# Query-key-norm attention and a soft mixture of experts: seven tokens of a head per partition, heads in fours, and fp32 loads of q, k and v by the hardware queue

## The chip, the cores and the metric

One core of a Trainium2 chip runs the whole program. The metric is the device time of one execution in microseconds (us), as the median of several. The profile's span is some 2 us shorter than that time (300.6 of 302.37 us before). Engines: PE is the matrix engine and PEld its weight loads, ACT evaluates functions (here the exponentials), DVE and POOL are the two elementwise engines, SP does nothing in these traces but issue transfers.

## The reference, cut to what matters

```python
# q, k, v: (8, 12, 448, 64) fp32
def rmsnorm(x, g):
    rms = np.sqrt(np.mean(x * x, axis=-1, keepdims=True) + 1e-06)
    return x / rms * g
q_n, k_n = rmsnorm(q, g_q), rmsnorm(k, g_k)
attn = softmax(q_n @ k_n.T / sqrt(64)) @ v            # 96 heads
x = attn.transpose(0, 2, 1, 3).reshape(3584, 768)
logits = x @ phi                                      # phi: (768, 32)
d = softmax(logits, axis=0); slot_input = d.T @ x     # 8 experts, 4 slots each
h = relu(slot_input[e] @ w1[e]); slot_out[e] = h @ w2[e]   # w1 768x1024, w2 1024x768
out = softmax(logits, axis=1) @ slot_out              # (3584, 768) fp32
```

The kernel reads 33 MB of q, k and v and 50 MB of expert weights, all fp32 (and 4.7 MB of the weights a second time, from a bf16 scratch), and computes in bf16. Attention fills most of the time; the expert weights (16 matrices of 3.1 MB) are fetched under it, so that the experts can start as soon as the last head is done.

## The kernel before

It puts four tokens of a head on each of 112 partitions (448 = 112 x 4) and works on pairs of heads. In this kernel all loads with a cast go through GpSimd's software queue (q0 of the page): q, k, v and the weights arrive in bf16 in one queue.

```python
P = 112; SI = 4; HU = 6; GU = HU // 2      # units of six heads, three pairs each
place("raw", 2 * HU * SI * D, 4)           # q and k of four units
place("vraw", HU * SI * D, 3)

def load(u, h0=0, h1=HU):                  # one unit, cast to bf16 on the way
    b, hb = u // 2, (u % 2) * HU
    for t, src in ((0, q), (1, k)):
        nc.gpsimd.dma_start(out=rawunit(u)[:, t, h0:h1],
                            in_=src[b, hb + h0:hb + h1].rearrange("h (p si) d -> p h (si d)", p=P))

def loadw(i):                              # one expert matrix
    if i in scratch:                       # the last three go by way of DRAM
        nc.sync.dma_start(out=wplace[i], in_=scratch[i])
    else:
        nc.gpsimd.dma_start(out=wt[i], in_=wsrc(i))

for g in range(-3, NG + 4):                # one pair of heads per step
    ...
    elif g + 6 < NG:
        square(g + 6)                      # ACT, or POOL for every third pair
    if 0 <= g + 2 < NG:
        scaleqk(g + 2)                     # POOL: q and k times 1/rms; frees raw
    ...
    if g >= 0 and g % GU == 1:
        u = g // GU
        if u + 4 < NU:
            load(u + 4)                    # first needed by square(3u + 12), at g = 3u + 6
        if u + 3 < NU:
            loadv(u + 3)
```

A unit is asked for five steps, 5 x 4.5 = 22.5 us, before its first use (21.7 to 23.9 us in the trace, from unit 5 on).

The softmax here doesn't subtract the row's maximum and nothing guards it: scores larger than these inputs give would overflow.

## Time and profile before

| | before |
|---|---|
| time | 300.09 us, median of 3 (298.52 to 300.27) |
| span of the profiled run (that execution took 302.37 us) | 300.6 us |
| first exponential starts, last one ends | 15.4, 230.24 us |
| first expert matmul | 239.08 us |
| experts, from there to the transposes of their outputs | 26.85 us |
| pace of attention | 9.0 us per four heads |

The views that bound the kernel (engines, windows, groups, chain) stand in the prediction below. The first two lines are from the table of waits: who waited for what; us in total, times, longest.

```profile
ACT arena L172 <- DMA arena<-in_k_dram: 6.0, 3, 3.6
...
POOL arena L199 <- DMA arena<-in_v_dram: 1.6, 1, 1.6
```

The next are from the page's tables of queues (packets, MB, share of 16 engines) and of transfers (number, KB each, median us from the request to the landing).

```profile
q0 software_dynamic: 48464, 41.73, 90.4%
q1 hardware_dynamic: 3056, 15.73, 12.9%
...
arena<-in_q_dram POOLq DMA_DIRECT2D x15, 336.0 KB, 6.7
arena<-in_k_dram POOLq DMA_DIRECT2D x15, 336.0 KB, 7.7
```

The hardware queue q1 carries only the output and the reloads from scratch. A load of q or k takes 6.7 or 7.7 us to land in the median (11.0 at most); the four waits of the first fence all lie before 21 us. (The 336 KB are what lands, in bf16; in fp32, each load reads 672 KB.)

### The profile page before, as it was taken

How to read it: one execution, taken by the hardware profiler on the slowest of the kernel's cores; microseconds unless marked ns; L12 is line 12 of the kernel's file. 1: busy time of each engine (PE TensorE's matmuls, PEld its weight loads, DVE VectorE, ACT ScalarE, POOL GpSimd, SP SyncE). 2: the span in 40 equal slices, each digit the busy share in tenths (PEclk: the TensorE clock that was granted, in tenths of full speed). 3: DMA queues.
4: the chain of work that ended last, by engine and by line, in shares of the span. 5: the costliest groups of instructions: out<-in, count | busy, mean ns of one | idle time of the engine just before them, and what ended most of it. 6: DMA issues, size and time to landing. Idle time of an engine off the chain costs nothing. (4 is left out here: it accounts for less than half of the span.)

```text
span 300.6 us, 8905 instructions
## 1 busy us (share of the span) xinstructions
PE 241.5 (80%) x3828; PEld 182.8 (61%) x3828; DVE 205.8 (68%) x407; ACT 216.2 (72%) x283; POOL 205.6 (68%) x233
## 2 busy tenths in 40 slices
PE   7469878989797898979789897989996776989900
PEld 3137556767685676758567675867875676854300
DVE  3575867978889897988989788888675410138800
ACT  3498996989998998999899899979986000026700
POOL 8879999989998998999999999977930000000000
PEclk9756995988999999999999989979999555555555
DMA  6999999999999999999999999999799991009996
GB/s 75 147 147 173 204 188 206 192 175 175 198 167 185 175 197 150 151 206 195 190 166 205 193 201 134 164 194 210 117 185 211 311 409 50 4 2 396 411 413 248
DMA packets 51558, 58.02 MB, mean 193 GB/s; under 512 B 2496, under 2 KB 42944, under 8 KB 51136
## 3 DMA queue, kind: packets, MB, share of 16 engines
q0 software_dynamic: 48464, 41.73, 90.4%
q1 hardware_dynamic: 3056, 15.73, 12.9%
q8 instruction: 30, 0.49, 0.6%
q14 instruction: 8, 0.07, 0.1%
HBM read 88.18 MB, written 15.73 MB: 346 GB/s over the span
## 5 line engine op out<-in xcount | busy, mean ns | idle before, releaser
L230 ACT ACTIVATE arena<-sc 112x896 bf16<-112x896 f32 x192 | 162.9, 916 | 14.1 <-PE sc L229 13.9
L229 PE MATMUL sc<-arena 128*112 128x448 bf16 x384 | 113.4, 379 | 15.4 <-ACT arena L230 13.3
L190 POOL TENSOR_TENSOR arena<-arena,rs 112x512 bf16<-112x512 bf16 x96 | 99.1, 1053 | 3.6 <-ACT rs L184 3.4
L240 PEld LDWEIGHTS <-arena 112*128 112x128 bf16 x1536 | 68.1, 100 | 28.5 <-issue 5.3
L178 DVE TENSOR_REDUCE ss<-arena 112x16 f32<-112x1024 f32 x48 | 58.4, 1219 | 26.4 <-ACT arena L172 21.7
L240 PE MATMUL ov<-arena 112*128 112x65 bf16 x1536 | 73.2, 197 | 1.8 <-DVE arena L252 1.4
L229 PEld LDWEIGHTS <-arena 128*112 128x112 bf16 x384 | 43.7, 137 | 21.5 <-issue 15.4
L172 ACT ACTIVATE arena<-arena 112x1024 f32<-112x1024 bf16 x34 | 35.8, 1052 | 6.1 <-DMA arena<-in_k_dram 6.0
L458 ACT ACTIVATE wown<-op,arena 128x768 f32<-128x768 f32 x14 | 12.4, 900 | 37.8 <-PE op L455 37.8
L199 POOL COPY arena<-arena 112x512 bf16<-112x512 bf16 x48 | 29.0, 604 | 13.1 <-PE ov L240 11.5
L218 PEld LDWEIGHTS <-arena 112*128 112x128 bf16 x384 | 25.6, 104 | 16.9 <-POOL arena L190 9.4
L218 PE MATMUL qkTp<-ident,arena 112*128 112x112 bf16 x384 | 30.5, 225 | 6.4 <-POOL arena L190 6.3
L252 DVE TENSOR_TENSOR arena<-ov,rd 128x512 bf16<-128x512 f32 x48 | 33.2, 691 | 1.7
L265 DVE COPY arena<-xTp 128x512 bf16<-128x512 bf16 x48 | 20.4, 425 | 9.6 <-PE xTp L264 8.5
L170 POOL TENSOR_TENSOR arena<-arena 112x1024 f32<-112x1024 bf16 x14 | 26.7, 1909 | 0.2
L219 DVE TENSOR_SCALAR arena<-qkTp,gg 128x448 bf16<-128x448 bf16 x48 | 21.5, 449 | 1.9 <-PE qkTp L218 1.3
L264 PE MATMUL xTp<-ident,arena 128*128 128x128 bf16 x192 | 19.1, 222 | 1.1 <-DVE arena L252 1.1
L221 DVE COPY arena<-qkTp 64x448 bf16<-64x448 bf16 x48 | 18.9, 395 | 1.2
L220 DVE COPY arena<-qkTp 64x448 bf16<-64x448 bf16 x48 | 17.9, 373 | 0.0
L460 DVE TENSOR_SCALAR wown<-op,arena 128x768 f32<-128x768 f32 x14 | 14.2, 1017 | 4.6 <-PE op L455 4.4
L454 PE MATMUL op<-arena,eT 32*128 32x512 bf16 x28 | 16.0, 617 | 1.4 <-ACT wown L458 0.7
L124 POOL DMA_DIRECT2D arena<-in_q_dram x18 | 14.3, 792 | 0.9 <-POOLq L478 0.9
(61 smaller groups left out, 208.2 us busy)
## 6 DMA issues: line engine op xcount, KB each, us to landing
wown<-in_moe_w_dram POOLq DMA_DIRECT2D x10, 1536.0 KB, 13.8
out_dram<-wown SPq DMA_DIRECT2D x12, 768.0 KB, 8.5
arena<-in_v_dram POOLq DMA_DIRECT2D x16, 336.0 KB, 8.9
arena<-in_q_dram POOLq DMA_DIRECT2D x15, 336.0 KB, 6.7
arena<-in_k_dram POOLq DMA_DIRECT2D x15, 336.0 KB, 7.7
scr<-in_moe_w_dram POOLq DMA_DIRECT2D x3, 1536.0 KB, 11.4
arena<-in_moe_w_dram POOLq DMA_DIRECT2D x3, 1536.0 KB, 13.1
arena<-scr SPq DMA_DIRECT2D x2, 1536.0 KB, 12.5
```

The costliest lines, as they stand in the source:

```text
L170: nc.gpsimd.tensor_tensor(sq, rawpair(p), rawpair(p), op=MUL)
L172: nc.scalar.activation(out=sq, in_=rawpair(p), func=ACTF.Square)
L178: nc.vector.reduce_sum(sss[p // GU][:, p % GU], at("sq", p).bitcast(F32).rearrange("p (r d) -> p r d", d=D), axis=AX)
L190: nc.gpsimd.tensor_tensor(qkn[:, t], rawpair(p)[:, t].rearrange("p h (s d) -> p s h d", d=D), rs[:, t].to_broadcast([P, SI, 2, D]), op=MUL)
L199: nc.gpsimd.tensor_copy(vext(p)[:, :, :, :D], vr[:, 2 * hp:2 * hp + 2])
L218: nc.tensor.transpose(pt[:, t, si * P:(si + 1) * P], qkn[:, t, si], ident[:P, :P])
L219: nc.vector.tensor_scalar(qT(p), pt[:, 0], gg, None, op0=MUL)
L229: nc.tensor.matmul(sc[:P, hh, :S], kT(p)[:, hh, i * P:(i + 1) * P], qT(p), start=True, stop=True)
L230: nc.scalar.activation(out=attn(p, i), in_=sc[:P, :, :S], func=ACTF.Exp, scale=0.125)
L240: nc.tensor.matmul(ovs[p][:, hh, c * (D + 1):(c + 1) * (D + 1)], attn(p, sik)[:, hh, C0[c]:C0[c] + 128], vext(p)[:, hh, sik, :D + 1], star ...
L252: nc.vector.tensor_tensor(x(b)[:, :, h * D:(h + 2) * D].rearrange("p c (h d) -> p h c d", d=D), o[:, :, :, :D], rd.to_broadcast([128, 2, 4 ...
L265: nc.vector.tensor_copy(xT(dc), xp)
```

## The change

Its intent: with 112 of 128 partitions in use, an eighth of every elementwise instruction is wasted (an exponential of 896 columns takes 916 ns on 112 partitions here). With seven tokens per partition, two heads fill 128 partitions (2 x 448 = 128 x 7), and a quad of four heads takes two such rows. q, k and v are loaded as fp32, without a cast; SP issues the loads on the hardware queue, and GpSimd is rid of 40 us of issuing (52 issues, 14.3, 13.5 and 12.4 us before). The keys come in chunks of 128; the fourth, of 64, is shared by two heads, which makes 7 exponentials per quad in place of 8. The buffers for q and k hold fp32 now, and there is one for each of three quads. The core of the diff:

```diff
-    place("raw", 2 * HU * SI * D, 4)
-    place("vraw", HU * SI * D, 3)
+    place("raw", 2 * 2 * 2 * NT * D, 3)
+    place("vraw", 2 * 2 * NT * D, 2)
 ...
-            nc.gpsimd.dma_start(out=rawunit(u)[:, t, h0:h1],
-                                in_=src[b, hb + h0:hb + h1].rearrange("h (p si) d -> p h (si d)", p=P))
+        src = (q, k)[t][Q // QB, Q % QB * 4:Q % QB * 4 + 4].rearrange("h t d -> (h t) d")
+        nc.sync.dma_start(out=raw(Q)[:, t], in_=src.rearrange("(r p s) d -> p r (s d)", r=2, s=NT))
 ...
+    def loadv(Q):                          # four transfers, of 1024- and 768-byte rows
+        for r in range(2):
+            ...
+            nc.sync.dma_start(out=vraw(Q)[0:64, ...], in_=src[:, :, :m])
+            nc.sync.dma_start(out=vraw(Q)[64:128, ...], in_=src[:, :, m:])
 ...
-        nc.vector.tensor_copy(eT[...].rearrange("n (p s) -> n s p", s=SI), ...)   # stride 4 elements
+        nc.vector.tensor_copy(eT[...].rearrange("n (p s) -> n s p", s=NT), ...)   # stride 7 elements
 ...
+    for Q in range(NQ + 2):                # the order within one quad, cut
+        if Q + 4 < NQ: load(Q + 4, 0); load(Q + 4, 1)      # SP
+        square(Q + 3, 0); square(Q + 3, 1, True)           # q on ACT, k on POOL
+        scaleqk(Q + 2, 0)                                  # POOL
+        vcopy(Q + 1); scaleqk(Q + 2, 1)                    # POOL
+        loadv(Q + 3)                                       # SP
+        while wnext < NPRE and Q >= wnext * 9 // 5: loadw(wnext); wnext += 1   # software queue
```

## The prediction

> **What bounds the kernel now.** I read the whole page first, then a table of windows, the chain of waits, and the groups of instructions.
>
> ```profile
> PE 241.5 (80%) x3828; PEld 182.8 (61%) x3828; DVE 205.8 (68%) x407; ACT 216.2 (72%) x283; POOL 205.6 (68%) x233
> ```
>
> No engine is full over the span, because the span has stages. The windows (busy time of each engine in each stretch) separate them:
>
> ```profile
> 0.00:15.00 15.00, 9.48 (x40) 3.88 (x40) 6.42 (x17) 6.00 (x9) 12.60 (x21) 0.87 0.92 111
> ...
> 120.00:150.00 30.00, 25.75 (x414) 19.84 (x413) 26.67 (x53) 28.37 (x38) 29.26 (x32) 1.00 1.18 184
> ...
> 250.00:262.00 12.00, 9.97 (x367) 9.90 (x367) 1.31 (x7) 0.00 (x0) 0.00 (x0) 0.50 0.02 5
> 262.00:280.00 18.00, 15.79 (x158) 9.08 (x156) 10.54 (x14) 8.42 (x10) 0.00 (x0) 0.50 0.53 212
> ```
>
> After the length come PE, PEld, DVE, ACT and POOL busy, PE clock, DMA share, GB/s. From about 20 to 230 us is attention: ACT 95% and POOL 98% busy, DVE 89%. ACT and POOL are both nearly full, so taking work from one alone would gain little. The last 60 us (expert layers, output) have nothing of the change in them. The chain of waits gives the pace: the router of two successive batches, six head pairs apart.
>
> ```profile
> 163.62 0.59 PE lg L271 x24
> ...
> 190.62 0.59 PE lg L271 x24
> ```
>
> That is 27.0 us for six pairs: 4.5 us per pair, 9.0 per four heads (a quad). 24 quads make 216 us. The groups that fill it:
>
> ```profile
> L230 ACT ACTIVATE arena<-sc 112x896 bf16<-112x896 f32 x192 | 162.9, 916 | 14.1 <-PE sc L229 13.9
> L190 POOL TENSOR_TENSOR arena<-arena,rs 112x512 bf16<-112x512 bf16 x96 | 99.1, 1053 | 3.6 <-ACT rs L184 3.4
> L178 DVE TENSOR_REDUCE ss<-arena 112x16 f32<-112x1024 f32 x48 | 58.4, 1219 | 26.4 <-ACT arena L172 21.7
> L172 ACT ACTIVATE arena<-arena 112x1024 f32<-112x1024 bf16 x34 | 35.8, 1052 | 6.1 <-DMA arena<-in_k_dram 6.0
> L199 POOL COPY arena<-arena 112x512 bf16<-112x512 bf16 x48 | 29.0, 604 | 13.1 <-PE ov L240 11.5
> L170 POOL TENSOR_TENSOR arena<-arena 112x1024 f32<-112x1024 bf16 x14 | 26.7, 1909 | 0.2
> L124 POOL DMA_DIRECT2D arena<-in_q_dram x18 | 14.3, 792 | 0.9 <-POOLq L478 0.9
> ```
>
> Every one of the ACT, DVE and POOL rows works on 112 partitions; an instruction's time depends on its columns, so an eighth of each is wasted. Back to back an exponential takes 162.9/192 = 0.848 us, less than its own 916 ns, because neighbours overlap. POOL also spends 18+18+16 issues of about 0.78 us, 40 us, on casting q/k/v loads.
>
> [...]512 columns take 425 ns in the bf16 transpose copy, 691 ns in the fp32 normalisation. [...]the trace's bf16 forms have 1.86 (1909/1024) and 2.06 (1053/512). It does not show all-fp32 inputs, which the change introduces: my largest unknown.[...]
>
> **The change, per quad (two pairs before, one quad after).**
>
> ACT. Before: 8 exponentials x 0.848 = 6.8; squares 34/24 x 1.05 = 1.5; logarithm and exponential of the norms and the router's exponential about 0.5. Sum 8.8 of 9.0. After: 168 exponentials in all, 7 x 0.848 = 5.94; [...]one logarithm/exponential pair about 0.5; router 0.1. Sum 7.5. Saved 1.3.
>
> DVE. Before: sums 2 x 1.22, query copies 2 x 0.45, key copies 2 x 0.77, transposed output 2 x 0.43, norms 2 x 0.90, router 1.6 per batch, /3 = 0.54. Sum 8.1. After: [...]key copies 2 x about 0.62; transposed output 0.69; norms unchanged 1.79; router 0.54. Sum 7.1.
>
> POOL. Before: scales 4 x 1.05 = 4.2, squares 14/24 x 1.91 = 1.1, v copies 1.2, q/k/v issues 40/24 = 1.7, weight issues 0.5. Sum 8.7. After: two scales and one square, 896 columns of fp32 each. The bf16 slope (1909-1053)/512 = 1.67 ns gives 1.05 + 384 x 1.67 = 1.69 us[...]. The v copy becomes four instructions (two of 384 columns, two of 128 on half the partitions): about 1.5, more than before, since each pays its fixed cost. Weight issues 0.55. Sum 7.7, with a span from 7.1 to 8.1.
>
> PE. The trace's busy hours have a pair of score matmuls at 0.40 us, an output matmul of 65 columns at about 0.033 and a transpose at 0.05. Before: 16 scores 3.2, 64 outputs 2.1, 24 transposes 1.3, router 0.55: 7.2. After: 14 scores 2.8, 48 outputs of 65 and 8 of 130 columns 2.1, 23 transposes 1.3, router 0.55: 6.75. Not the bound at full clock.
>
> DMA. The bytes read stay 88 MB. Before, attention reads about twice the 184 GB/s that it lands, some 370; the peak slices land 210, so 420. A quad needs 1.38 MB of q/k/v and on average 1.7 MB of weights: 3.1 MB in 8 us is 385 GB/s, close under that.
>
> Pace. ACT alone was busy for 8.8 of 9.0. With ACT at 7.5, POOL at 7.7 and DVE at 7.1, in program order and within 8% of each other, I allow 5% of waiting: 8.05 us per quad. The last three quads have no squares left: 7.3.
>
> Start. Before, the first exponential ran at 15.4 us. After: q and k of the first quad (0.9 MB) by about 5 us; two squares, sums and norms to 7.8; scale 9; transposes and copies 11.7. But both squares and the norm of the second quad stand ahead of the first exponential on ACT, and their row sums stand behind the copies on DVE: 14.5. The first quad carries three extra squares and two norms, and POOL's backlog: it ends at 27.4.
>
> Sum: 27.4 + 20 x 8.05 + 3 x 7.3 = 210.3 for the last exponential. The chain from there to the first expert matmul (last outputs, norm, transposes, router, its copies) took 239.1 - 230.2 = 8.9 before; slightly less after, 8.3: 218.6. The expert layers and output took 300.6 - 239.1 = 61.5 and are unchanged; I add 0.7 for weights that come late. 280.8 of span, so 280 us.
>
> **Rivals.**
> 1. *POOL becomes the bound.* If an all-fp32 operation takes 2.0 us or more, POOL needs 8.1, and the pace is 8.3 to 8.4: +6, about 287. For it: POOL's present 98%[...], four copies in place of two. Against it: 40 us of issues leave POOL.
> 2. *The weights come late.* The change asks for seven weight matrices (3.1 MB each to read) in quads 17 to 22, with the last q/k/v: some 26 MB, 65 us at 400 GB/s. These begin near 163 us and end near 228, the reloads from scratch near 238, while the experts want the last ones from 231 to 241. One interruption more makes 3 to 8 us: 284 to 288. Before, the loads were over at 250 and expert work ran to 265, so there was slack; most of it goes.
> [...]
> 4. *ACT sets a clean pace* of 7.6 with no added waits: about 271.
>
> **Range and chances.** The pace carries nearly everything: 0.3 us per quad is 7 us. Rivals 1 and 2 push up, rival 4 down. 271 to 291, eight times in ten. Faster by over 2% means under 294.1; slower would need a pace over 9.2, which only a serious stall of loads could make. Faster 0.91, same 0.07, slower 0.02.
>
> **What would show it.** Right: the exponentials 168, about 142 us; the all-fp32 POOL rows near 1.9 us; fp32 sums 1.085 us; query copy near 0.68 us; first exponential near 14.5, last near 210, first expert matmul near 219; three router marks 24 us apart. Wrong: a POOL row over 2.1 us with POOL at 98%; ACT waiting for scores for more than 10% of attention; the key copies over 0.9 us; gaps of more than 1 us between expert layers beyond those of before, which point to weights; or squares that wait for loads in mid-attention.

Passages that rested on figures from outside are cut, terms of the forecast's sum among them: one square on ACT, the sums and the query copy on DVE, the two scales and the square on POOL. With them the sums per quad came to 7.5, 7.1 and 7.7 us; without them the terms left give 6.54, 4.26 and 2.05. So 0.95, 2.85 and 5.6 us, and with them the 8.05 of the pace and the 280.8 of the span, were the author's estimates and rest in part on what no trace had shown. The trace after has 945 ns for the square on ACT, 1085 for each of the two sums, 676 for the query copy, 1713 for each scale and 1682 for the square on POOL. The terms that stand without a source measure 617 ns (key copies, 0.62) and 680 (transposed output, 0.69); the 1.9 us near the end for POOL's fp32 rows is such an estimate too. Where a number's subject is cut with it, the 1.86 and 2.06 are POOL's, in ns an element. Also cut is the third rival: that the long copies out of PSUM become slower, for about 290 us. Two statements stand that the traces show with these numbers. Time goes by columns and not by partitions: an exponential of 896 columns took 916 ns on 112 partitions and 914 on 128, and POOL's products of 512 and 1024 columns 1053 and 1909 ns. And each copy of v has a fixed cost: in the trace after they take 501 and 507 ns for 384 columns, and still 288 and 292 for 128.

## The result, and the profile after

The changed kernel took 330.61 us (median of 4 runs, 329.9 to 331.05) beside 299.97 of the kernel before on the same chip: a ratio of 1.103, 95% interval 1.0987 to 1.1072. Ratios here are the mean time of one kernel's fast runs over that of the other's of the same rounds, so they are not quite the ratio of the medians. It is correct.

| | before | predicted | after |
|---|---|---|---|
| span | 300.6 | 280.8 | 329.2 |
| first exponential starts | 15.4 | 14.5 | 16.52 |
| last exponential ends | 230.24 | 210.3 | 261.7 |
| first expert matmul | 239.08 | 218.6 | 270.36 |
| us per quad in the middle | 9.0 | 8.05 | 10.51 |

(The pace after is the time between ACT's squares of quads 4 and 23, over 19 quads.) Everything was lost in attention. Its end moved by 31.5 us; what follows the first expert matmul gave back 2.7, most of it among the experts (24.4 us in place of 26.85), and the span grew by 28.6.

The engines' busy time, and the window that the prediction showed of before:

```profile
PE 234.6 (71%) x3564; PEld 167.0 (51%) x3564; DVE 192.0 (58%) x315; ACT 193.6 (59%) x268; POOL 164.4 (50%) x187
```

```profile
120.00:150.00 30.00, 16.82 (x244) 12.00 (x242) 17.23 (x27) 16.30 (x23) 17.23 (x19) 0.92 1.04 238
```

In these 30 us ACT is busy for 16.3 (28.4 before), POOL for 17.2 (29.3 before), DVE for 17.2: no engine is the bound. (These are 30 bad microseconds, with two long stalls in them. From 16 to 262 us ACT is busy 71% of the time, POOL 65% and DVE 64%.) The work did shrink, as the groups show (busy us, mean ns of one, then idle time before them and what ended it):

```profile
L252 ACT ACTIVATE arena<-sc 128x896 bf16<-128x896 f32 x168 | 147.4, 914 | 31.8 <-PE sc L251 31.1
...
L195 DVE TENSOR_REDUCE ss<-arena 128x14 f32<-128x896 f32 x48 | 52.0, 1085 | 67.7 <-ACT arena L189 59.9
L207 POOL TENSOR_TENSOR arena<-arena,rs 128x896 bf16<-128x896 f32 x47 | 80.5, 1713 | 13.1 <-ACT rs L200 6.9
L187 POOL TENSOR_TENSOR arena<-arena 128x896 f32<-128x896 f32 x21 | 35.3, 1682 | 67.4 <-DMA arena<-in_k_dram 27.5
...
L189 ACT ACTIVATE arena<-arena 128x896 f32<-128x896 f32 x27 | 25.5, 945 | 37.3 <-DMA arena<-in_q_dram 35.3
...
L319 DVE COPY eT<-eTp 32x448 bf16<-32x448 bf16 x8 | 15.2, 1901 | 0.2
```

The last two columns are the news. The squares of q (L189) and of k (L187) stood behind 37.3 and 67.4 us of idle time, and what ended most of it was a load. The table of waits names them (all but one wait of 2.2 us for q lie in mid-attention):

```profile
ACT arena L189 <- DMA arena<-in_q_dram: 35.3, 11, 6.7
...
POOL arena L187 <- DMA arena<-in_k_dram: 27.5, 6, 6.7
...
POOL arena L187 <- DMA arena<-in_v_dram: 17.9, 3, 7.7
```

The last line needs care, as a square of k reads no v. The profile infers what ended a wait from the last semaphore event before it, and that can be the wrong one. In all 13 waits of L187 (named after k, v, PE or DVE), the square starts 0.1 to 0.2 us after the load of its own k has landed; in the three of the last line, k lands at 90.90, 187.69 and 220.80 us and the squares start at 91.04, 187.83 and 220.94. So all 67.4 us of L187 are waits for k, and with L189's the squares wait 104.7 us for loads. Waits of squares are counted in this way below.

The shares of the chain that ended last, by engine, before and then after:

```profile
PE 26%; ACT 14%; DVE 5%; issue 3%; ACTq 0%
```

```profile
DMA 31%; PE 30%; DVE 11%; ACT 10%; POOL 8%; issue 4%; SPq 2%; ACTq 0%; POOLq 0%
```

Transfers now hold 31% of the span on the chain. Before they held none, but there the chain could be followed back only to 141 us, so it says nothing of the first half. The queues and the transfers:

```profile
q1 hardware_dynamic: 29616, 48.77, 47.1%
q0 software_dynamic: 15376, 25.22, 43.2%
...
arena<-in_q_dram SPq DMA_DIRECT2D x24, 448.0 KB, 9.1
arena<-in_k_dram SPq DMA_DIRECT2D x24, 448.0 KB, 10.6
```

q, k and v lie on q1 now, the weights alone on q0, and a load takes 9 to 11 us. Here is one stall in order of time (start, us, engine, what; in brackets the idle time before it and what ended that), first from SP's timeline, then from ACT's:

```profile
125.54 0.61 SPq L129 DMA_DIRECT2D arena<-in_v_dram  x1
126.20 0.60 SPq L130 DMA_DIRECT2D arena<-in_v_dram  x1
126.85 0.60 SPq L129 DMA_DIRECT2D arena<-in_v_dram  x1
127.55 0.59 SPq L130 DMA_DIRECT2D arena<-in_v_dram  x1
128.24 0.54 SPq L118 DMA_DIRECT2D arena<-in_q_dram  x1
```

```profile
137.76 0.90 ACT L252 ACTIVATE arena<-sc 128x896 bf16<-128x896 f32 x1
145.35 0.95 ACT L189 ACTIVATE arena<-arena 128x896 f32<-128x896 f32 x1 [6.68 <-DMA arena<-in_q_dram]
```

SP issues four loads of v, 0.6 us each, when POOL has copied the v before it, and only then the load of q. That one is requested at 128.24 and lands just before 145.35, 17.1 us later; ACT had been idle for 6.68 us.

**The theory.** It has two factors. First, *the lead is short*: load(Q+4) is asked for at the head of step Q and its square stands at the head of step Q+1, one quad later, where before it was 22.5 us. Its buffer is that of quad Q+1, so it cannot be asked for before POOL has scaled that quad, in step Q-1; in the code the loads of v still come between. In the trace POOL keeps the program's order (L187, L207, L214 to L217, L207, three times from 98 to 128 us, with 8.36 us of idle time before the second L187), and that scaling stands behind a square that itself waits for a load, so by the program's order a late load delays the request after next too. From the requests of q to the squares that use them I read a median of 10.1 us and a minimum of 7.8 (quads 6 to 23; the square's own wait is in it). Second, *the landing is long* (9.1 and 10.6 us in the median), because the weights share the 16 DMA engines with it (without them, in e1, it takes 3.9 and 4.8). Counted from the trace's records of transfers, for the stall above (bytes read; packets as the records have them):

```
us        q0 (weights)            q1 (q, k, v)
124-128   334 GB/s, 435 packets    67 GB/s, 221 packets
128-132   251 GB/s, 327 packets   141 GB/s, 330 packets
132-136   301 GB/s, 330 packets    96 GB/s, 326 packets
136-140   327 GB/s, 319 packets    61 GB/s, 320 packets
140-144   222 GB/s, 232 packets   174 GB/s, 443 packets
144-148     0 GB/s,   1 packet    291 GB/s, 991 packets
```

While both queues have work (126 to 142 us here), each gets about the same number of packets, so bytes follow the size of a packet: the weights' rows read 4096 or 3072 bytes, those of q and k 1792, those of v 1024 and 768. Over 30 to 215 us there are 108 microseconds in which each queue starts at least 20 packets of data: 76.8 of the weights and 78.8 of q, k and v in the mean, but 268 GB/s and 111. The equal counts don't hold at every moment: at 123 and 124 us q1 had a request pending and moved nothing. Then, with the weights landed and the loads of the quad too, little is requested: 35 of these 185 us read under 200 GB/s, 15 before. The mean is 314 GB/s, against 359 before in the same stretch. By what rule the engines pass from one queue to the other, the records don't show.

**Rivals.** (a) The loads are late only because they are slow: a fairer share alone would do. (b) Only the order on SP's queue, with v ahead, makes them late. (c) The elementwise work is slower than its busy time shows, so the pace would be near 10 without any load being late.

### The profile page after: what moved, and what is told of

Its sections match the earlier page's. It is cut to its first block, busy times and chain, and to the rows that moved or that the text cites. A ratio compares the mean times of both kernels' runs of the same rounds, so it can differ in the third digit from the quotient of the medians.

```text
span 329.2 us, 8387 instructions
## 1 busy us (share of the span) xinstructions
PE 234.6 (71%) x3564; PEld 167.0 (51%) x3564; DVE 192.0 (58%) x315; ACT 193.6 (59%) x268; POOL 164.4 (50%) x187
## 4 chain that ended last, share of the span: by engine, by line
DMA 31%; PE 30%; DVE 11%; ACT 10%; POOL 8%; issue 4%; SPq 2%; ACTq 0%; POOLq 0%
DMA arena<-in_q_dram 22%; PE ov L265 7%; PE sc L251 7%; ACT arena L252 6%; DMA arena<-in_k_dram 6%; POOL arena L207 4%; DVE eT L319 3%; PE hTp L472 3%; PE soTp L481 3%; PE op L511 3%; DVE arena L276 3%; PE qkTp L225 2%; ACT arena L189 2%; DMA g<-in_g_q_dram 2%; POOL arena L187 2%
## 5 line engine op out<-in xcount | busy, mean ns | idle before, releaser
L252 ACT ACTIVATE arena<-sc 128x896 bf16<-128x896 f32 x168 | 147.4, 914 | 31.8 <-PE sc L251 31.1
L251 PE MATMUL sc<-arena 128*128 128x448 bf16 x336 | 101.6, 388 | 39.1 <-ACT arena L252 38.4
L265 PEld LDWEIGHTS <-arena 128*128 128x128 bf16 x1344 | 64.9, 104 | 63.3 <-DVE arena L276 32.2
L265 PE MATMUL ov<-arena 128*128 128x65 bf16 (+1 forms) x1344 | 72.6, 207 | 27.8 <-DVE arena L276 27.7
L195 DVE TENSOR_REDUCE ss<-arena 128x14 f32<-128x896 f32 x48 | 52.0, 1085 | 67.7 <-ACT arena L189 59.9
L207 POOL TENSOR_TENSOR arena<-arena,rs 128x896 bf16<-128x896 f32 x47 | 80.5, 1713 | 13.1 <-ACT rs L200 6.9
L187 POOL TENSOR_TENSOR arena<-arena 128x896 f32<-128x896 f32 x21 | 35.3, 1682 | 67.4 <-DMA arena<-in_k_dram 27.5
L251 PEld LDWEIGHTS <-arena 128*128 128x128 bf16 x336 | 26.7, 104 | 43.7 <-issue 41.7
L189 ACT ACTIVATE arena<-arena 128x896 f32<-128x896 f32 x27 | 25.5, 945 | 37.3 <-DMA arena<-in_q_dram 35.3
L225 PE MATMUL qkTp<-ident,arena 128*128 128x128 bf16 x360 | 32.6, 241 | 2.2 <-DVE arena L207 1.1
L515 ACT ACTIVATE wown<-op,arena 128x768 f32<-128x768 f32 x14 | 12.4, 899 | 35.9 <-PE op L512 35.9
L225 PEld LDWEIGHTS <-arena 128*128 128x128 bf16 x360 | 26.2, 109 | 9.7 <-POOL arena L207 3.2
L236 DVE COPY arena<-qkTp 64x896 bf16<-64x896 bf16 x48 | 29.6, 617 | 1.3 <-PE qkTp L225 0.4
L517 DVE TENSOR_SCALAR wown<-op,arena 128x768 f32<-128x768 f32 x14 | 14.2, 1017 | 4.6 <-PE op L512 4.4
L290 DVE COPY arena<-xTp 128x1024 bf16<-128x1024 bf16 x24 | 16.3, 680 | 0.7 <-PE xTp L287 0.7
L287 PE MATMUL xTp<-ident,arena 128*128 128x128 bf16 x192 | 14.6, 219 | 1.4 <-DVE arena L276 1.0
L287 PEld LDWEIGHTS <-arena 128*128 128x128 bf16 x192 | 12.7, 98 | 5.9 <-DVE arena L276 1.2
L319 DVE COPY eT<-eTp 32x448 bf16<-32x448 bf16 x8 | 15.2, 1901 | 0.2
## 6 DMA issues: line engine op xcount, KB each, us to landing
arena<-in_k_dram SPq DMA_DIRECT2D x24, 448.0 KB, 10.6
```

What stands on the lines that cost most here:

```text
L187: nc.gpsimd.tensor_tensor(sq(t), r, r, op=MUL)
L189: nc.scalar.activation(out=sq(t), in_=r, func=ACTF.Square)
L195: nc.vector.reduce_sum(sss[Q][:, t], sq(t).rearrange("p (r d) -> p r d", d=D), axis=AX)
L207: (eng or nc.gpsimd).tensor_tensor(qkn(Q, t).rearrange("p s (r d) -> p s r d", r=2), raw(Q)[:, t].rearrange("p r (s d) -> p s r d", d=D), ...
L225: nc.tensor.transpose(pts[t][:, i], qkn(Q, t)[:, s], ident)
L236: nc.vector.tensor_copy(kT(Q)[r, :, hh].rearrange("p w (s c) -> p w s c", s=NT), pt[r, :, 1 - hh:8 - hh])
```

## The experiments

Twelve kernels ran. "Pace" is always that between ACT's squares of quads 4 and 23, "lead" the median from a request of q to its square, "landing" the median of q and of k. The lead runs to the square as it ran, so the square's own wait is in it. The first six kernels ran once each. The kernel before took 299.4 to 300.0 us beside all of them (medians).

| run | time, us | pace | lead | landing q, k | last exponential ends |
|---|---|---|---|---|---|
| changed kernel | 330.6 | 10.51 | 10.1 | 9.1, 10.6 | 261.7 |
| e1_weights_late | 384.7 | 8.28 | 10.8 | 3.9, 4.8 | 218.9 |
| e3_scale_first | 301.1 | 8.82 | 14.2 | 10.9, 12.6 | 229.6 |
| e4_qk_before_v | 305.2 | 8.86 | 12.7 | 9.2, 8.7 | 234.8 |
| e5_small_packets | 307.0 | 9.01 | 8.2 | 7.6, 8.9 | 233.1 |
| e6_four_buffers_mended | 298.5 | 8.57 | 14.6 | 9.1, 9.7 | 224.0 |
| e7_four_and_scale_first | 305.0 | 8.92 | 22.3 | 11.1, 12.3 | 231.1 |
| e8_plain_eT | 302.3 | 8.78 | 21.0 | 10.9, 12.1 | 226.1 |
| e9_halves_spaced | 292.5 | 8.16 | 16.6 | 10.2, 12.2 | 216.9 |
| e10_three_halves | 295.4 | 8.47 | 11.4 | 9.3, 8.7 | 219.4 |
| e11_four_plain_eT | 298.5 | 8.49 | 14.1 | 9.1, 10.0 | 220.0 |
| e12_one_queue_end | 290.9 | 8.16 | 17.4 | 10.4, 11.9 | 216.4 |

### e1_weights_late: attention without the weights beside it

Every weight load moves behind attention; nothing else changes.

```diff
-        while wnext < NPRE and Q >= wnext * 9 // 5:
+        while wnext < NPRE and Q >= NQ:
             loadw(wnext)
 ...   # the casts to scratch and the loads of the last three steps: all at Q == NQ
```

> All 16 expert weights are requested only after the last quad; buffers, order and q/k/v loads stay as in the changed kernel, whose squares ran 10.5 us per quad apart. Theory A (lead too short: a q/k load can only be requested when the POOL has scaled the quad three before, about one quad ahead of its use, and the landing then takes 9 to 17 us): without weights a q/k pair should land in 4 to 5 us after its request, so the waits for in_q and in_k (65 us in the changed kernel) fall under 10 us, the pace falls to about 8.1 us and the last exponential ends near 218 instead of 258 us. Rival B (bandwidth as such: fp32 landing is too much for the DMA engines): attention would speed up too, but q/k landings would stay near 9 us. Rival C (only the order of requests on the sync queue, behind the v loads, holds it): pace stays at 10 us. The total is no use here: the weights then take some 130 us alone, near 400 us.

Measured: 384.67 us (one run; correct). The total is of no interest, as the weights come afterwards with nothing to hide them. Attention ends at 218.9, at a pace of 8.28.

```profile
arena<-in_q_dram SPq DMA_DIRECT2D x24, 448.0 KB, 3.9
arena<-in_k_dram SPq DMA_DIRECT2D x24, 448.0 KB, 4.8
```

The requests come with the lead of the changed kernel (10.8 us), but land in less than half the time. Squares wait for loads for 8.4 us in all, where they had waited for 104.7. So rival (c) falls: the elementwise work, in this order, runs at 8.28, within 3% of the predicted 8.05, if its data are there. It also shows that the contention is with the weights.

### e2_four_buffers: one more buffer for q and k (failed)

Four quads of raw buffers, one weight fewer that has a place of its own, and load(Q+5) at the head of step Q.

```diff
-    NPRE = 10
+    NPRE = 9
-    place("raw", 2 * 2 * 2 * NT * D, 3)
+    place("raw", 2 * 2 * 2 * NT * D, 4)
-        if Q + 4 < NQ or Q == 0:
-            ...load(Q + 4)
+        for qn in ((3, 4, 5) if Q == 0 else (Q + 5,)):
+            if qn < NQ: load(qn, 0); load(qn, 1)
-        if Q in (NQ - 4, NQ - 3, NQ - 2):
-            loadw(NPRE + Q - (NQ - 4))
+        if Q in (NQ - 5, NQ - 4, NQ - 3, NQ - 2):
+            loadw(NPRE + Q - (NQ - 5))
```

> Four buffers of raw q/k in place of three (one own weight place given up for the room), each load requested one quad earlier, weights in the loop as before. Theory A: two quads of lead (about 16 us) cover nearly every landing, waits for in_q and in_k fall from 65 to under 15 us, pace 8.2 to 8.6, total 283 to 293 us. Rival B: bandwidth binds, so the landings only get longer, pace stays near 10, total 320 to 330 us. Rival D ([...]q/k/v cannot get their 170 GB/s on average): a part of the waits stays, 300 to 315 us.

The result was wrong (relative error 0.077), and it is my mistake: the weights that are loaded into spent buffers of q and k started one step too early, and one overwrote the last quad before it was scaled. POOL waited 25.0 us for that weight, so the 314.38 us say nothing. From quad 4 to 20 the pace was 8.59. Mended as e6 below.

### e3_scale_first: free the buffer sooner

Three buffers stay. POOL scales quad Q+2 before it squares quad Q+3, and the load into the freed buffer follows at once.

```diff
+        elif Q + 2 < NQ:                   # head of step Q
+            scaleqk(Q + 2, 0)
+            scaleqk(Q + 2, 1)
+            if Q + 5 < NQ:
+                load(Q + 5, 0)
+                load(Q + 5, 1)
 ...   # the two scaleqk(Q + 2) later in the step go
```

> Three buffers as in the changed kernel; the POOL scales quad Q+2 at the start of quad Q instead of after the square of quad Q+3, which waits for a load, and the load of quad Q+5 is requested right behind it. Theory A says that what matters is the lead: the request then comes about two quads ahead of use without any more memory, and no longer hangs behind the wait for another load. Total 283 to 295 us, waits for in_q and in_k under 15 us. Rival B: 320 to 330 us. If the buffer count itself mattered, no gain here while e2 gains.

Measured: 301.09 us (one run; correct), short of what I hoped but 29.5 better than the changed kernel, from a change of order alone. It holds the order of e4 too (q and k ahead of v), so only the 4 us between e3 and e4 are left for the sooner release, and both are single runs. The lead grows to 14.2 us, although the landing becomes no shorter (10.9 and 12.6). So rival (a), that only the share matters, falls. Part of what is missing shows in the copies of v: with q and k ahead of v, these now wait 18.0 us for their loads (1.8 in the changed kernel).

### e4_qk_before_v: only the order on SP's queue

The release stays as it was; load(Q+5) is issued before loadv(Q+3) instead of after it.

```diff
+        if 0 < Q and Q + 5 < NQ:
+            load(Q + 5, 0)
+            load(Q + 5, 1)
         if Q + 3 < NQ:
             loadv(Q + 3) if Q else (loadv(2), loadv(3))
```

> Only the order on the sync queue: the q/k load of the next quad is requested ahead of the four v loads (2.6 us of issue), its release unchanged. Rival C (order of requests is the cause): total under 300 us. Theory A: the request comes 1 to 2 us earlier of the 8 to 10 that are missing, so 315 to 327 us.

Measured: 305.24 us (one run; correct), better than I gave it: I had rated this order too low. Four issues of v take 2.7 us (125.54 to 128.24 above), and the 448 KB of v that they put ahead, at 111 GB/s, take about 4 more (an estimate from those two numbers). Rival (b) is half right: the v ahead is much of the short lead, but the squares still wait for loads, 43.0 us for q and k in all, and the copies of v 15.9. How the gain splits between the issues and the bytes ahead was not separated.

### e5_small_packets: only the share

Buffers and order stay; each weight load is cut into two halves of its columns, so that its rows read 2048 or 1536 bytes.

```diff
-            nc.gpsimd.dma_start(out=wt[i], in_=wsrc(i))
+            n = wsrc(i).shape[2] // 2
+            nc.gpsimd.dma_start(out=wt[i][:, :, :n], in_=wsrc(i)[:, :, :n])
+            nc.gpsimd.dma_start(out=wt[i][:, :, n:], in_=wsrc(i)[:, :, n:])
```

> The changed kernel with each weight load cut in two, so that one weight packet reads 2 KB or 1.5 KB in place of 4 or 3 KB; buffers, requests and order of q/k/v untouched. Theory D (while both queues have work [...]big weight packets crowd out the 1.8 KB q/k packets): in stretches with both queues busy the q/k/v queue should rise from about 110 to 150-180 GB/s, q/k landings fall from 9.1 and 10.6 us to 7-8 us, and the total from 330 to 305-320 us. If the split of bandwidth did not matter (only the lead or the order), no change: 327 to 336 us.

Measured: 306.96 us (one run; correct), as expected. With both queues busy (counted as above) the weights read 211 GB/s and q, k and v 148, where it had been 268 and 111. Nothing in the order of requests changed, no byte was saved, the measured lead even fell to 8.2 us, and 24 us came back. That is the most direct evidence that the size of the other queue's packets sets the share. It does not bring the pace to 8.2: more lead or more share is still missing, and this run doesn't say which.

### e6_four_buffers_mended: a quad more of lead

As e2, but the weight that needs the place of the last quad waits for it:

```diff
+        for i, qi in enumerate((NQ - 5, NQ - 3, NQ - 3, NQ - 2)):
+            if Q == qi:
+                loadw(NPRE + i)
```

> The four-buffer kernel with my mistake mended (a weight was loaded over the last raw buffer one quad too early, which gave a wrong result and a 25 us wait at the end). The request order on the sync queue is as in the changed kernel. Theory A (lead): the pace of 8.45 us per quad that the first try showed up to quad 20 goes on to the end, 288 to 296 us, correct. If the order of requests behind v were a separate cause that more lead does not heal, it would stay above 303 us, as with the q/k-first kernel.

Measured: 298.47 us (one run; correct), above the 288 to 296 expected; lead 14.6, pace 8.57. Attention ends 6 us before that of the kernel before, but the experts then take 29.1 us in place of 26.85. PE waits only 0.36 us of that for a load of weights; 6.65 us are gaps of the kind described under e12, of which the kernel before had 4.95.

### e7_four_and_scale_first: both leads together (a miss)

```diff
-        for qn in ((3, 4, 5) if Q == 0 else (Q + 5,)):
+        elif Q + 2 < NQ:
+            scaleqk(Q + 2, 0)
+            scaleqk(Q + 2, 1)
+            if Q + 6 < NQ: load(Q + 6, 0); load(Q + 6, 1)
```

> Four buffers, scaling first on the POOL, q/k requested right behind the scaling and ahead of v: about three quads of lead. Theory A: the pace reaches that of the kernel without weights in the loop (8.2 us), last exponential at 219 to 224 us, total 287 to 294 us. If bandwidth bounds, it does not get under the better of the two parts (299 us).

Measured: 305.03 us, ratio 1.0175 (1.0115 to 1.0235: unclear, at a threshold of 2%). I had expected 287 to 294. The lead is 22.3 us, that of the kernel before, yet it is slower than e6. The waits say why:

```profile
POOL arena L215 <- DMA arena<-in_v_dram: 10.7, 7, 3.5
```

Squares wait for almost nothing now; the copies of v do. With q and k asked for that early, v stands behind them in the same queue, beside weights whose packets are as large as before. More lead for one load took it from another here.

### e8_plain_eT: the transposed weights of the router with long runs

On top of e7, the one instruction that the prediction had missed: the copy L319 writes single 2-byte elements 14 bytes apart. The token's place within its partition becomes the slow index, so the copy writes runs of 64, and the readers follow.

```diff
-        nc.vector.tensor_copy(eT[r, b % 2 * S:b % 2 * S + S].rearrange("n (p s) -> n s p", s=NT),
+        nc.vector.tensor_copy(eT[r].rearrange("n (s b p) -> n b s p", s=NT, b=2)[:, b % 2],
 ...
-        return eT[NS * j:NS * (j + 1)].rearrange("n (p s) -> n s p", s=SO)[:, s]
+        return eT[NS * j:NS * (j + 1), s * 128:(s + 1) * 128]
```

> As the one before, and the transposed router weights are stored with token position as the slow index, so that the copy writes runs of 64 instead of single bf16 elements 14 bytes apart. The copy (1901 ns in the changed kernel, 1158 ns before) should take 0.4 to 0.7 us, eight times; it stands in front of the output norm on VectorE, so 4 to 10 us of time: 280 to 289 us. If it lies beside other work, no more than 2 us of gain over the one before.

Measured: 302.34 us, ratio 1.0095 (1.0015 to 1.0175), that is 2.7 us less than e7 of the same rounds, where I had expected 280 to 289.

### e9_halves_spaced: lead, share and the plain copy

From e6: weight loads in halves, one half every 0.9 quads, and the plain copy of e8.

```diff
-        while wnext < NPRE and Q >= wnext * 9 // 5:
-            loadw(wnext)
+        while wnext < 2 * NPRE and Q >= wnext * 9 // 10:
+            loadw(wnext // 2, (wnext % 2,))
             wnext += 1
```

> Three cures together on the four-buffer kernel (298.5 us in one run): weight loads cut in halves with packets of at most 2 KB, the halves requested one by one every 0.9 quad, and the router weights stored so that their copy writes runs of 64. If late q/k/v loads are the whole of what the changed kernel lost, attention should come close to the pace without weights in the loop (8.2 us, last exponential 217 to 221 us), and the total to 286 to 293 us, faster than before by 2 to 4 per cent. If the DMA engines' bandwidth is the next bound (88 MB to read at some 390 GB/s are 226 us), what attention gains the expert layers wait for, and the total stays at 294 to 299 us.

Measured: 292.48 us, ratio 0.9759 (0.9696 to 0.9823): 7.4 us less than before, though the interval doesn't lie wholly past 2%, so the verdict is unclear. The pace is 8.16, the last exponential ends at 216.9, and reads have a mean of 364 GB/s, above the 359 of the kernel before. Here is what is left, in the experts, from PE's timeline:

```profile
249.49 0.80 PE L474 MATMUL hTp<-arena 128*128 128x4 bf16 x24 [2.86 <-DMA arena<-in_moe_w_dram]
```

The experts take 31.9 us in place of 26.85. This wait for weights is 2.9 of the 5.0; gaps of the kind described under e12 take 7.0 us, 2.0 more than before. Between 220 and 235 us the reloads from scratch, with 12 KB packets on the hardware queue, read 278 to 371 GB/s and leave 54 to 142 to the last weights on the software queue, which are wanted first: the same mechanism, with the sides exchanged.

### e10_three_halves: the share without the fourth buffer

The edits of e9, on e4 (three buffers, q and k before v) in place of e6:

```diff
     place("raw", 2 * 2 * 2 * NT * D, 3)
-        while wnext < NPRE and Q >= wnext * 9 // 5:
-            loadw(wnext)
+        while wnext < 2 * NPRE and Q >= wnext * 9 // 10:
+            loadw(wnext // 2, (wnext % 2,))
 ...   # halves in loadw and castw, the copy of e8
```

> The same weight halves and router copy with three buffers only, q/k requested ahead of v (305 us in one run with whole weights). Lead and share of the DMA engines can each make up for the other: with the share raised the short lead should nearly do, 290 to 298 us. If buffers are needed whatever the share, 300 us or more.

Measured: 295.39 us, ratio 0.9847 (0.9794 to 0.99). With three buffers and a lead of only 11.4 us it does better than e11 below, which has four buffers, a lead of 14.1, the same plain copy, and whole weights: there 298.5. Here too, lead and share stand in for one another.

### e11_four_plain_eT: the plain copy on e6 alone

```diff
-        nc.vector.tensor_copy(eT[r, b % 2 * S:b % 2 * S + S].rearrange("n (p s) -> n s p", s=NT),
+        nc.vector.tensor_copy(eT[r].rearrange("n (s b p) -> n b s p", s=NT, b=2)[:, b % 2],
 ...   # and the readers, as in e8
```

> The four-buffer kernel with nothing but the other storing of the router weights. The copy falls from 1.9 to about 0.5 us, eight times, ahead of the output norm on VectorE: 293 to 297 us against 298.5. If it lies beside other work, 297 to 300.

Measured: 298.5 us, ratio 0.9984 (0.9901 to 1.0066), no better than e6, although the copy fell to a fifth:

```profile
L319 DVE COPY eT<-eTp 32x448 bf16<-32x448 bf16 x8 | 3.1, 387 | 0.4 <-PE eTp L317 0.2
```

The last exponential comes 4 us earlier than in e6, and the experts take 33.0 us, 3.8 more than there: PE waits 3.9 us for a load of weights, in place of 0.4.

### e12_one_queue_end: the reloads behind the weights in one queue

From e9, one word: the reloads from scratch go on the software queue, where they stand behind the weights that are wanted before them.

```diff
-            nc.sync.dma_start(out=wplace[i], in_=scratch[i])
+            nc.gpsimd.dma_start(out=wplace[i], in_=scratch[i])
```

> Edit, from the kernel with four raw buffers, halved and spaced weight loads and the plain eT copy (292.5 us): the three reloads of expert weights from scratch leave the sync queue (hardware) and go on GpSimd's software queue, behind the two weight loads that are still in it. Theory (the queue with the larger packets takes the larger share; within one queue, what was asked for first comes first): in that kernel the reloads' large packets took 330 to 390 GB/s between 220 and 234 us and left about 50 to the two weights that the middle experts wait for. In one queue these two come first, the waits and gaps among the experts shrink from 31.9 us (first expert matmul to the transposes of the slots' outputs) to 27 to 29, and the total is 287 to 290. Pace and last exponential unchanged (8.1 to 8.2 us per quad; 216 to 218). Rival (total bytes are what the experts wait for, or the gaps are not waits for weights at all): no change, 291.5 to 293.5, only the expert that waits is another one.

Measured: 290.9 us (6 runs, 289.14 to 292.13), ratio 0.9716 (0.9679 to 0.9753): faster than both kernels, just above the range. The window of mid-attention has all three engines near 26 us of 30 (DVE 24), as the prediction had imagined the changed kernel:

```profile
120.00:150.00 30.00, 25.86 (x416) 18.75 (x414) 23.77 (x41) 26.70 (x38) 26.02 (x30) 1.00 1.18 262
```

No expert waits for a load of weights any more, but they still take 30.9 us, not the 27 to 29 expected. What remains are four gaps that the profile puts down to no semaphore:

```profile
230.05 0.56 PE L474 MATMUL hTp<-arena,wown 128*128 128x4 bf16 x15 [1.70 <-issue]
...
235.97 0.99 PE L483 MATMUL soTp<-arena,wown 128*128 128x4 bf16 x31 [2.35 <-issue]
...
241.87 1.42 PE L474 MATMUL hTp<-arena 128*128 128x4 bf16 x48 [2.35 <-issue]
...
247.68 0.62 PE L474 MATMUL hTp<-arena 128*128 128x4 bf16 x18 [2.31 <-issue]
```

They come every 126 to 128 matmuls, each with its weight load, hence every 256 instructions or just under, and before the end of each the trace has a transfer of 16384 bytes on the queue for instructions (at 227.75, 233.68, 239.55 and 245.30 us, each about 0.97 long). In the changed kernel the same gaps are 0.39, 1.25 and 0.17 us. Without these gaps the experts take 30.9 - 8.7 = 22.2 us here and 24.4 - 1.8 = 22.6 there. Before the change four such gaps sum to 5.0, and 26.85 less that is 21.9. So my reading, which no run shows, is that PE waits for its instructions, whose transfers wait behind weights that fill the DMA engines. The traces of all runs but e1 have 44 such gaps, and each ends 1.2 to 1.6 us after such a transfer has ended. Where the data queues read over 300 GB/s in the 6 us before its end, a gap takes 1.57 to 2.92 us (28 of 29); under 100 GB/s, 0.16 to 0.55 (all 9). One doesn't fit: the 0.39 of the changed kernel, at 371 GB/s. No run moved one of these transfers, so it stays argued.

## Why the prediction was wrong

**The step that failed** is under "Pace": "ACT alone was busy for 8.8 of 9.0. With ACT at 7.5, POOL at 7.7 and DVE at 7.1, in program order and within 8% of each other, I allow 5% of waiting: 8.05 us per quad." It took for granted that the loads are there. Nowhere does the prediction work out when a load may be asked for and how long it then takes. Both were to be had: one quad of lead, 8 us, from the order in the diff, and 6.7 and 7.7 us of landing from the profile of before, where one queue had the engines to itself (for 672 KB read, against 448 after). That has hardly any slack even if nothing gets slower. The runs put in its place a pace of 10.51, made of a clean one of 8.2 to 8.3 (e1, e9, e12) and 2.3 us of stalls, which a longer lead (e3, e4, e6), a fairer share (e5), or weights out of the way (e1) each take away for the most part.

The starting point was also read a little too full: 95, 98 and 89% are the shares of ACT, POOL and DVE in one window of 30 us. From 20 to 230 us they are 92, 90 and 82%, so ACT was busy for 8.25 of 9.0 us per quad, not 8.8, and idle for 8% of the time already. Two slips carry nothing: 23 transposes at 0.05 are 1.15 and not 1.3, and quads 17 to 22 ask for six weight matrices, as the seventh is asked for at the end of quad 16.

**"DMA"** compared bytes with capacity, 385 GB/s with 420, and stopped there. The capacity is there: e12 reads 365 GB/s in the mean from 30 to 215 us, at a pace of 8.16. What was not asked is who gets it. The one queue of before served requests in their order (its 69 loads land in that order). With two, each moved about as many packets as the other while both were busy (76.8 and 78.8 a microsecond), and the one with the small packets lost (111 GB/s against 268). The profile of before had a case of it: from 236 to 242 us the last weights on q0 and the reloads from scratch, in 12 KB packets on q1, moved 168 and 152 packets of data, but 115 and 311 GB/s.

**Rival 2** had the right players and the wrong victim: "The weights come late". The weights came early and q, k and v late. It came true in part once the stalls were cured: among the experts, PE waits for loads of weights for 2.0 to 3.9 us in e8 to e11.

**The components** were mostly right. The same 896 columns took 916 ns on 112 partitions and 914 on 128. There are 168 exponentials of 914 ns, 147.4 us (142 predicted). The fp32 scale on POOL takes 1713 ns and the square 1682; I took 1.88 us, an estimate that no trace had shown, and the bf16 slope's 1.69 would have been right. Rival 1 thus had no ground. The sums take 1085 ns as predicted, the query copy 676 (0.68), the key copies 617 (0.62), so the rival of slower copies falls as well. e1 and e12 confirm their sum: 8.28 and 8.16 beside 8.05. Rival 4, a clean pace of 7.6, never showed.

**Missed**: the copy into eT. It keeps its count and its size, so it looked unchanged, but its stride goes from 8 to 14 bytes and its time from 1158 to 1901 ns. Eight of them are 5.9 us of DVE. It was worth 2.7 us in e8 against e7, and nothing in e11, where weights had become the bound.

**Start and end**: the first exponential at 16.52 against 14.5 predicted. From the last exponential to the first expert matmul it took 8.6 us (8.3 predicted), and from there to the end 58.8 (62.2 predicted).

**"slower would need a pace over 9.2, which only a serious stall of loads could make"**: that is what happened. The prediction gives it 0.02 and no reason. In the kernel before, no wait for a load shows after 21 us; but what was hidden there was hidden by 22.5 us of lead, and the change takes that away. The sign that the prediction names last, "squares that wait for loads in mid-attention", showed. So did another, ACT waiting for scores for more than 10% of attention (31.1 of 245 us, 13%).

**Left open**: how e4's gain splits between v's issues and v's bytes; how e9's splits between halves and spacing; what the second queue alone cost, as no run put q, k and v of the changed kernel back on the weights' queue; and the transfers of instructions as the cause of the gaps among the experts.

## What to carry to other kernels

For every load of a changed loop, write down two numbers before anything else: the time from its request (which is when its buffer is freed, by the engine that frees it, in that engine's order, and behind what stands in the issuing queue) to its first use, and the time that it takes to land beside everything else that is being read. A profile without waits for loads says only that the old lead covered the old landing. And moving loads to another queue gave up their order here (111 GB/s for q, k and v, 268 for the weights): if a stream that is wanted now shares the engines with a bulk stream, keep them in one queue (e12 shows it for the reloads: no expert waits for a load of weights, where one waited 2.86 us in e9; for q, k and v it was not tried), or make the bulk stream's packets small (e5, 330.6 to 307.0 us) and its requests spaced (tried only together with that, in e9 and e10).
